# Pooled attention and a gated MLP: maxima of the late heads turned one head at a time, under a new order

## The chip, the cores and the metric

The kernel runs on one core of one Trainium2 chip, as one launch. The metric is the device time of a run in microseconds (us). Three runs of the kernel before gave 902.53, 903.97 and 904.75 us, a median of 903.97.

## The reference

The inputs are q, k and v (4 batches, 8 heads, 1152 positions, 64 channels, fp32) and the two weights of an MLP (512 x 2048 and 2048 x 512).

```python
q_pool = q.reshape(B, H, S // 2, 2, D).mean(axis=3)          # 576 pooled queries
scores = scale * np.matmul(q_pool, k.transpose(0, 1, 3, 2))  # 576 x 1152 per head
scores = scores - np.max(scores, axis=-1, keepdims=True)
attn = np.exp(scores)
attn = attn / (np.sum(attn, axis=-1, keepdims=True) + 1e-09)
x = np.matmul(attn, v)        # then heads side by side: 2304 x 512
h = x @ w_in
g = h * np.clip(h + 3.0, 0.0, 6.0) / 6.0
out = g @ w_out
```

The softmax needs the maximum of each pooled query over all 1152 keys. In the kernel the scores lie with the keys on the partitions and the queries along the free dimension, so this maximum runs over nine key tiles (elementwise, on VectorE) and then across the 128 partitions (which needs a transposition).

## The kernel before

**Tiling.** The heads are taken in pairs: 16 pairs `g`, four for each batch. A pair has two halves of 288 queries (`h`), and in each of these two heads (`j`). Pairs 0 to 4 (`g < EARLY`) are the first part: fp32 scores of both heads at once, in PSUM rooms called `v`. Pairs 5 to 15 are the late part: the scores are two matmuls of a split into a high and a low word, one head at a time. Beside the first part the MLP weights are converted from the raw words into a high and a low half (`convert`, L599, seven steps on ScalarE, GpSimd and VectorE for each of 32 pieces). The MLP takes the tokens in chunks of 256, 16 steps of the hidden dimension each. Six chunks lie among the late pairs; the last 768 tokens follow in a loop at the end (L866 on).

**The maximum of a late head.** `scores` (L398) leaves a key tile in PSUM. ScalarE copies it to the SBUF tile `s` (`keep`, L417), VectorE keeps the running maximum `m` (`most`, L424), 128 x 288 for each head. For the two heads of one `(g, h)` then follow, in the kernel before:

- `cross_m` (L431), ScalarE, once a head: 64 partitions of the head's `m` are copied into the other 64 partitions of a PSUM tile `pst`.
- `join_m` (L439), VectorE, once a head: the maximum of these and of the head's own 64 partitions, into `pm`. After both, `pm` holds head 0 in partitions 0 to 63 and head 1 in 64 to 127.
- `fold` (L444), TensorE, once for both heads: three transpositions of 128 x 96 of `pm` into `pst`.
- `best` (L450), VectorE, once for both: a maximum over 64 elements, six results to a partition, `mq`.
- `spread` (L457), TensorE, once a head: three transpositions that lay `mq` along the free dimension of all partitions, into a fresh `pst`.
- `lessen` (L467), VectorE, three a head: subtracts it from the 128 x 864 blocks of `s`. `expo` (L476), ScalarE, follows.

The early heads have no `cross_m` and `join_m`: `fold` and `best` run once a head on `m` itself, with a maximum over 128 elements and three results, and `spread` writes into the tile that `fold` used. The tile `pst` is one PSUM bank, `st` in the planner. The sums of the exponentials go another way (`total` L480, `cross_d` L504, `join_d` L511, `sums` L517): GpSimd adds, ScalarE carries one head's 64 partitions over, GpSimd joins.

**What sets the order.** The class `Order` (L37) is a planner that runs while the kernel is built. Each step has a place (a number that is its priority), the engines that may take it with a busy and an end time, steps that it needs, and rooms (buffers) that it takes and frees. The planner goes through time; a free engine takes, of the steps whose needs are met and whose rooms are free, the one with the lowest place. What it yields is the order of issue on every engine, TensorE, VectorE, ScalarE, GpSimd and the queue of SyncE (SP) that starts nearly all DMAs. Each engine then works through its own list in order. The places come from constants at L20 to L34: `PER` (places for one pair, early and late), `AT` and `ATL` (shifts of each kind of step, early and late), `CONV` and `CSTEP` (weight conversion), `START` and `SLOPE` (MLP chunks), `LAG` and `MLP` (steps inside the MLP), `BIAS` (how readily a step goes to its second engine). The planner's steps of the maximum are `mp`, `mc`, `s1`, `s2`, `s3`, `su` (L748 to L766). `second` (L815) is the border between the parts: it waits for all early scores and for the conversion of 12 of the 16 weight blocks.

Of the kernel before, what the change touches and what calls it, by code (L numbers as in the profile page):

```python
# [11 lines left out]
F32 = mybir.dt.float32  # L12
# [6 lines left out]


SBUFS = 3
START = (94.79, 128.23, 169.33, 204.1, 247.91, 270.62)
SLOPE = (2.19, 3.02, 2.72, 2.51, 1.78, 3.47)
LAG, MLP = 9.42, (2.56, -1.5, 4.75, 1.71)
CONV, CSTEP = 27.2, (39.17, 25.6)
NEAR = 5
EARLY, FCV = 5, 12
CVB = 1
BIAS = (-3.16, 165.7, 1.3, -2.73, 8.4, 2.65)
CUT = 8  # L30
PER = (18.24, 19.02)
AT = (1.82, 3.28, -1.17, 8.45, 1.17, 16.24, 17.65, 6.2, 8.03, -0.11, 4.3, 2.83, -21.04, 27.48)
ATL = (0.23, 5.42, -4.41, 15.94, 13.8, 18.37, 11.77, 34.99, -2.44, 15.27, 4.54, 6.0, -6.43, -6.01)
TAIL = 768  # L34


# [90 lines left out]
def pooled_attention_then_gated_mlp(ctx, tc, q, k, v, w_in, w_out, out):  # L127
# [128 lines left out]
    with ExitStack() as a:  # L256
# [171 lines left out]
        def halves(j):  # L428
            return slice(j * D, (j + 1) * D), slice((1 - j) * D, (2 - j) * D)

        def cross_m(eng, u):  # L431
            g, h, j = u
            if j == 0:
                st_t["x", g, h] = ps_st.tile([P, TQ * P], F32, tag="m", name="pst")
                m_t["p", g, h] = sm.tile([P, HQ], F32, tag="pm", name="pm", bufs=2)
            mine, other = halves(j)
            copy(eng, st_t["x", g, h][mine, 0:HQ], m_t[g, h][other, j])

        def join_m(eng, u):  # L439
            g, h, j = u  # L440
            mine, _ = halves(j)
            nc.vector.tensor_tensor(out=m_t["p", g, h][mine], in0=st_t["x", g, h][mine, 0:HQ], in1=m_t[g, h][mine, j], op=ALU.max)
# [236 lines left out]
        room = dict(kr=1, qr=1, qp=1, vr=2, kT=2, v=3, q=2, mb=2, pm=2, dh=2, s=3, S=SBUFS, m=2, st=1, d=2, av=1, x=2, xo=2,  # L679
                    raw0=1, raw1=1, size0=1, size1=1, wd0=1, wd1=1, mx=2, w0=3, w1=3, h=1, r6=2, g=3, o0=1, o1=1, ob=2)  # L680
        od = Order(room)
        add = od.add
# [6 lines left out]
        for g in range(NG):  # L689
# [34 lines left out]
            for h in range(NH):  # L724
                for j in range(2):
                    u = (g, h, j)
                    z0 = place(g) + UNIT * (2 * h + j)
                    tag = "s" if late else "v"
                    if late or j == 0:
                        before = (g, h, 0) if j else (g, h - 1, late) if h else (g - 1, NH - 1, g - 1 >= EARLY) if g else None  # L730
                        for t in range(KT):
                            end = t == KT - 1
                            z = z0 + UNIT / KT * t * (1 if late else 2)
                            add(("mm", u, t), z, {"PE": (268, 480) if late else (760, 980)}, partial(scores, u=u, t=t),
                                ([("mm", u, t - 1)] if t else [("mm", before, KT - 1)] if before else [])
                                + ([("ql", g, h, j) if late else ("qh", g, 0, 0)] if not t else []) + [("kl", g, t // KC) if late else ("kh", g, t // 6)]
                                + ([("second",)] if late and not t else []),
                                (tag,), (("q",) * (j if late else h) + ("kT",) * (h == NH - 1 and j == late)) if end else ())
                            first = not t and not j
                            add(("cp", u, t), z, {"ACT": (300, 400) if late else (505, 605)}, partial(keep, u=u, t=t),  # L740
                                [("mm", u, t)] + ([("cp", u, t - 1)] if t else []), ("S", "m") if first else (), () if t else (tag,))
                            if t:
                                add(("mx", u, t), z + .1, {"DVE": (368, 450) if late else (668, 750)}, partial(most, u=u, t=t),
                                    [("cp", u, t)] + ([("mx", u, t - 1)] if t > 1 else []), (), (tag,))
                    w = u if late else (g, h, 0)
                    last = [("mx", w, KT - 1)]
                    z = z0 + (UNIT if late or j else 2 * UNIT)
                    if late:  # L748
                        add(("mp", u), z + at[8], {"ACT": (300, 400)}, partial(cross_m, u=u), [("mx", (g, h, n), KT - 1) for n in range(2)] if late else last, () if j else ("pm", "st"))
                        add(("mc", u), z + at[8], {"DVE": (370, 450)}, partial(join_m, u=u), [("mp", u)] + [("mc", (g, h, 0))] * j, (), ("m", "st") if j else ())  # L750
                        if j:
                            p = (g, h)
                            add(("s1", p), z + at[2], {"PE": (330, 550)}, partial(fold, u=p), [("mc", (g, h, n)) for n in range(2)], ("st",), ("pm",))
                            add(("s2", p), z + at[2], {"DVE": (474, 550)}, partial(best, u=p), [("s1", p)], (), ("st",))
                            for n in range(2):
                                add(("s3", (g, h, n)), z + at[2] + n, {"PE": (250, 470)}, partial(spread, u=(g, h, n)), [("s2", p)] + [("s3", (g, h, 0))] * n, ("st",))
                    else:
                        add(("s1", u), z + at[2], {"PE": (330, 550)}, partial(fold, u=u), last, ("st",), ("m",) if j else ())
                        add(("s2", u), z + at[2], {"DVE": (474, 550)}, partial(best, u=u), [("s1", u)])
                        add(("s3", u), z + at[2], {"PE": (250, 470)}, partial(spread, u=u), [("s2", u)])  # L760
                        add(("sb", u), z + at[2], {"ACT": (300, 400)}, partial(keep_m, u=u), [("s3", u)], ("mb",))
                    for c in C3:
                        add(("su", u, c), z + at[3] + c, {"DVE": (970, 1045)} if late else {"DVE": (970, 1045), "POOL": (2000, 2050, BIAS[0])}, partial(lessen, u=u, c=c),
                            [("s3", u) if late else ("sb", u)] + ([("su", u, c - 1)] if c and late else []), (),
                            (("st",) if c == 2 else ()) if late else (("st", u, 3), ("mb", u, 3)))
                        add(("ex", u, c), z + at[3] + 1 + c, {"ACT": (831, 930)}, partial(expo, u=u, c=c), [("su", u, c)])  # L766
                    for n in range(4 if late else 0):
                        cost = 2000 if n < 2 else 765
                        add(("ad", u, n), z + at[4] + 1.5 * n, {"POOL": (cost, cost + 50)}, partial(total, u=u, n=n),
                            [("ex", u, c) for c in (range(2) if n == 0 else (2,) if n == 1 else ())] + ([("ad", u, n - 1)] if n else []),  # L770
                            () if n else ("d",), (("S", u[:2], 3),) if n == 1 else ())
                    if late:
                        add(("dx", u), z + at[7], {"ACT": (300, 400)}, partial(cross_d, u=u), [("ad", u, 3)], () if j else ("dh",))
                        add(("dj", u), z + at[7], {"POOL": (765, 815)}, partial(join_d, u=u), [("dx", u)], (), ("d",))
# [147 lines left out]
```

## Time and profile before

| what | value |
|---|---|
| median of 3 runs | 903.97 us |
| the profiled execution, its own time | 904.39 us |
| its span, first to last instruction | 902.5 us |
| mean granted clock of TensorE | 0.987 |
| TensorE matmuls busy (PE) | 863.0 us, 96% |
| TensorE weight loads busy (PEld) | 671.9 us, 74% |
| VectorE busy (DVE) | 638.4 us, 71% |
| ScalarE busy (ACT) | 618.4 us, 69% |
| GpSimd busy (POOL) | 523.4 us, 58% |

The profile is of one execution; 1.9 us of its time lie outside its span. Matmuls are pipelined and the end of one is modelled, so the busy time of PE is that of overlapping records; how closely the starts follow each other tells how full the engine is. The granted clock is given as a share of 2.4 GHz: a stretch at 1.00 ran at 2.4 GHz, one at 0.50 at 1.2 GHz, and a value between is a mean over both.

### The profile page before, as it was taken

The numbers are of one execution on the slowest core, as the hardware profiler recorded it, in microseconds if no ns is written. First come the engines' busy times: TensorE is split into PE (matmuls) and PEld (weight loads), VectorE is DVE, ScalarE is ACT, GpSimd is POOL, SyncE is SP. The second block draws the span as 40 slices with busy tenths as digits, with TensorE's granted clock in tenths as the row PEclk, the third lists the DMA queues.
The fourth block names the chain that finished last, engine by engine and source line by source line (L and its number), as shares of the span: only waits on it lengthen the run. The fifth ranks groups of instructions, "written<-read, shape, count | busy, mean of one in ns | idle before, by whom it ended". The sixth has DMA issues, their size and how long they took to land.

```text
span 902.5 us, 16987 instructions
## 1 busy us (share of the span) xinstructions
PE 863.0 (96%) x5976; PEld 671.9 (74%) x5976; DVE 638.4 (71%) x1196; ACT 618.4 (69%) x1320; POOL 523.4 (58%) x474
## 2 busy tenths in 40 slices
PE   4889989989999999999999999999999999999997
PEld 3445445457778887889888888888888877888886
DVE  5879989887898888777877777787876761322222
ACT  4878888875778888878777787787876763222222
POOL 2556747444567888867686977677885695000000
PEclk9889999999999999999999999999999999999999
DMA  9978576469988777769686787787678658534433
GB/s 261 277 225 257 201 232 218 156 205 303 323 273 276 222 234 207 245 218 320 213 246 214 223 280 236 266 273 250 221 262 273 198 189 282 181 121 135 138 96 93
DMA packets 113396, 204.00 MB, mean 226 GB/s; under 512 B 44448, under 2 KB 68000, under 8 KB 113312
## 3 DMA queue, kind: packets, MB, share of 16 engines
q1 hardware_dynamic: 112624, 201.55, 70.1%
q10 hardware_dynamic: 688, 1.38, 0.5%
q8 instruction: 47, 0.77, 0.4%
q14 instruction: 37, 0.30, 0.1%
HBM read 171.97 MB, written 30.93 MB: 225 GB/s over the span
## 4 chain that ended last, share of the span: by engine, by line
PE 75%; DMA 7%; DVE 7%; ACT 5%; issue 3%; POOL 2%; SPq 0%; DVEq 0%; ACTq 0%; POOLq 0%
PE ph L183 21%; PE po L216 16%; PE pav L495 12%; PE pqk L408 12%; PE pt L216 5%; DVE m L426 3%; DMA raw<-in_moe_w_in_dram 2%; DMA raw<-in_moe_w_out_dram 2%; PE pst L465 2%; ACT s L310 2%; PE pt L382 1%; DMA qr<-in_q_dram 1%; ACT s L478 1%; DMA w_d<-scratch 1%; PE psr L521 1%
## 5 line engine op out<-in xcount | busy, mean ns | idle before, releaser
L470 DVE TENSOR_TENSOR s<-s,pst 128x864 f32<-128x864 f32 x168 | 173.8, 1047 | 32.6 <-PE pst L465 27.4
L478 ACT ACTIVATE s<-s 128x864 f32<-128x864 f32 x192 | 176.7, 933 | 24.6 <-DVE s L470 22.6
L183 PE MATMUL ph<-mxmxh,w 128*128 128x256 f32 x896 | 181.0, 285 | 0.0
L426 DVE TENSOR_TENSOR m<-pqk,m 128x288 f32<-128x288 f32 x308 | 139.6, 453 | 38.2 <-ACT s L310 27.0
L495 PE MATMUL pav<-s,vr 128*64 128x288 f32 x1152 | 156.6, 417 | 0.0
L310 ACT COPY s<-pqk 128x288 f32<-128x288 f32 x396 | 145.9, 400 | 14.3 <-PE pqk L408 10.8
L183 PEld LDWEIGHTS ph<-mxmxh,w 128*128 128x128 f32 x896 | 146.5, 190 | 2.2 <-issue 0.9
L216 PE MATMUL po<-w,gh 128*128 128x512 f32 x448 | 139.3, 392 | 0.0
L188 ACT ACTIVATE r<-ph,three 128x256 f32<-128x256 f32 (+1 forms) x128 | 64.1, 501 | 102.1 <-PE ph L183 98.2
L183 PE MATMUL ph<-mxmxl,w 128*128 128x256 f32 x448 | 126.4, 282 | 0.0
L408 PE MATMUL pqk<-qh,kT 128*128 128x288 f32 x396 | 124.2, 327 | 2.2 <-DVE m L426 1.0
L488 POOL TENSOR_TENSOR d<-s 128x864 f32<-128x864 f32 x44 | 90.1, 2048 | 58.1 <-ACT s L478 55.2
L495 PEld LDWEIGHTS pav<-s,vr 128*64 128x64 f32 x1152 | 78.1, 138 | 59.1 <-issue 11.1
L192 DVE SCALAR_TENSOR_TENSOR r<-r,ph 128x256 f32<-128x256 f32 (+1 forms) x128 | 57.5, 449 | 90.2 <-ACT r L188 89.7
L408 PE MATMUL pqk<-ql,kT 128*128 128x288 f32 x396 | 111.6, 294 | 0.0
L201 POOL TENSOR_TENSOR gl<-r,gh 128x256 fp32r<-128x256 f32 x96 | 70.9, 738 | 52.1 <-ACT gh L196 34.1
L216 PEld LDWEIGHTS po<-w,gh 128*128 128x128 f32 x448 | 84.3, 188 | 14.5
L216 PE MATMUL po<-w,gl 128*128 128x512 f32 x224 | 90.0, 402 | 1.5 <-DMA w<-w_d 1.5
L488 POOL TENSOR_TENSOR d<-d,s 128x864 f32<-128x864 f32 x44 | 90.3, 2051 | 0.6
L408 PEld LDWEIGHTS pqk<-qh,kT 128*128 128x128 f32 x396 | 74.6, 188 | 17.8 <-DVE m L426 5.2
L183 PEld LDWEIGHTS ph<-mxmxl,w 128*128 128x128 f32 x448 | 85.2, 190 | 0.8
L196 ACT CAST gh<-r 128x256 fp32r<-128x256 f32 (+1 forms) x128 | 55.7, 435 | 39.3 <-DVE r L192 26.7
(97 smaller groups left out, 1500.7 us busy)
## 6 DMA issues: line engine op xcount, KB each, us to landing
w<-w_d SPq DMA_DIRECT2D x224, 512.0 KB, 5.0
w_d<-scratch SPq DMA_DIRECT2D x32, 512.0 KB, 5.5
kr<-in_k_dram SPq DMA_DIRECT2D x32, 288.0 KB, 5.0
vr<-in_v_dram SPq DMA_DIRECT2D x16, 576.0 KB, 4.0
qr<-in_q_dram SPq DMA_DIRECT2D x15, 576.0 KB, 6.8
raw<-in_moe_w_in_dram SPq DMA_DIRECT2D x16, 512.0 KB, 5.3
raw<-in_moe_w_out_dram SPq DMA_DIRECT2D x16, 512.0 KB, 5.1
xh_d<-xh SPq DMA_DIRECT2D x32, 144.0 KB, 4.8
```

The costliest lines, as they stand in the source:

```text
L183: nc.tensor.matmul(ps, w[:, wi, cs], x[:, c, :], start=(m == 0), stop=(m == 3 * NCC - 1))
L188: nc.scalar.activation(out=r6, in_=ps, func=AF.Relu, bias=three)
L192: nc.vector.scalar_tensor_tensor(out=out, in0=r6, scalar=6.0, in1=ps, op0=ALU.min, op1=ALU.mult)
L201: on.tensor_tensor(out=gl, in0=r6, in1=gh.bitcast(F32), op=ALU.subtract)
L216: nc.tensor.matmul(o, g[:, ts], w[:, wi, :], start=(f == 0 and n == 0), stop=(f == NFC - 1 and n == 2))
L310: nc.scalar.copy(out=out, in_=in_)
L408: nc.tensor.matmul(ps[:, 0:HQ], kT[g][:, j, t, :], w[:, j, :], start=(m == 0), stop=(m == 1))
L426: nc.vector.tensor_tensor(out=m, in0=ps, in1=s0 if t == 1 else m, op=ALU.max)
L470: by[eng].tensor_tensor(out=s, in0=s, in1=m.unsqueeze(1).to_broadcast([P, KC, HQ]), op=ALU.subtract)
L478: nc.scalar.activation(out=s, in_=s, func=AF.Exp, scale=SCALE)
L488: by[eng].tensor_tensor(out=out, in0=x, in1=y, op=ALU.add)
L495: nc.tensor.matmul(av_t[g, h][j * D:(j + 1) * D, :], vr_t[g][:, j, t, :], s_t[g, h][:, j, t, :], start=(t == 0), stop=(t == KT - 1),)
```

## The change

For the late pairs `cross_m` and `join_m` go, with their tiles. `fold`, `best` and `spread` are now the same for early and late: once a head, on `m` itself, and `spread` writes into the tile of `fold`. The sums of the two heads are still joined. All constants of the order are new; the costs in the planner are the same ones. The cut diff:

```diff
-START = (94.79, 128.23, 169.33, 204.1, 247.91, 270.62)
-SLOPE = (2.19, 3.02, 2.72, 2.51, 1.78, 3.47)
-LAG, MLP = 9.42, (2.56, -1.5, 4.75, 1.71)
-CONV, CSTEP = 27.2, (39.17, 25.6)
+START = (107.21, 129.44, 181.69, 204.5, 238.8, 274.39)
+SLOPE = (2.16, 3.08, 1.38, 1.98, 2.64, 2.75)
+LAG, MLP = 7.8, (2.55, -3.98, 15.46, 2.58)
+CONV, CSTEP = 20.06, (51.27, -5.14)
...
-BIAS = (-3.16, 165.7, 1.3, -2.73, 8.4, 2.65)
+BIAS = (-4.9, 201.89, 3.95, -7.11, 17.98, 9.02)
 CUT = 8
-PER = (18.24, 19.02)
-AT = (1.82, 3.28, -1.17, 8.45, 1.17, 16.24, 17.65, 6.2, 8.03, -0.11, 4.3, 2.83, -21.04, 27.48)
-ATL = (0.23, 5.42, -4.41, 15.94, 13.8, 18.37, 11.77, 34.99, -2.44, 15.27, 4.54, 6.0, -6.43, -6.01)
+PER = (18.27, 18.6)
+AT = (1.61, 2.63, -2.01, 12.09, -1.48, 16.23, 12.27, 2.3, 6.72, -1.57, 5.33, 2.34, -49.57, -29.1)
+ATL = (-0.35, 5.1, -1.26, 35.67, 13.02, 16.99, 7.49, 56.73, -0.96, 4.9, 4.35, 18.93, -19.18, -7.86)
...
-        def cross_m(eng, u):
...
-        def join_m(eng, u):
...
         def fold(eng, u):
             st = st_t[u] = ps_st.tile([P, TQ, P], F32, tag="m", name="pst")
-            m = m_t[u[:2]][:, u[2]] if len(u) > 2 else m_t.pop(("p",) + u)
+            m = m_t[u[:2]][:, u[2]].rearrange("p (t q) -> p t q", q=QP)
             for x in range(TQ):
-                nc.tensor.transpose(st[:QP, x, :], m[:, x * QP:(x + 1) * QP], ident)
+                nc.tensor.transpose(st[:QP, x, :], m[:, x, :], ident)
 
         def best(eng, u):
-            n = 1 if len(u) > 2 else 2
-            mq = sm.tile([QP, TQ * n], F32, tag=f"mq{n}", name="mq")
-            nc.vector.tensor_reduce(out=mq, in_=st_t[u][:QP].rearrange("p x (j k) -> p (x j) k", j=n), axis=AX.X, op=ALU.max)
-            for j in range(n):
-                m_t["q", u if n == 1 else u + (j,)] = mq[:, j::n]
+            m_t["q", u] = sm.tile([QP, TQ], F32, tag="mq", name="mq")
+            nc.vector.tensor_reduce(out=m_t["q", u], in_=st_t[u][:QP], axis=AX.X, op=ALU.max)
 
         def spread(eng, u):
             mq = m_t.pop(("q", u))
-            if u[0] < EARLY:
-                st = st_t[u].rearrange("p x k -> p (x k)")[:, 0:HQ]
-            else:
-                st = ps_st.tile([P, TQ * P], F32, tag="m", name="pst")[:, 0:HQ]
-            st_t[u] = st
+            st = st_t[u] = st_t[u].rearrange("p x k -> p (x k)")[:, 0:HQ]
...
-                    if late:
-                        add(("mp", u), z + at[8], {"ACT": (300, 400)}, partial(cross_m, u=u), [("mx", (g, h, n), KT - 1) for n in range(2)] if late else last, () if j else ("pm", "st"))
-                        add(("mc", u), z + at[8], {"DVE": (370, 450)}, partial(join_m, u=u), [("mp", u)] + [("mc", (g, h, 0))] * j, (), ("m", "st") if j else ())
-                        if j:
...
-                    else:
...
+                    add(("s1", u), z + at[2], {"PE": (330, 550)}, partial(fold, u=u), last, ("st",), ("m",) if j else ())
+                    add(("s2", u), z + at[2], {"DVE": (474, 550)}, partial(best, u=u), [("s1", u)])
+                    add(("s3", u), z + at[2], {"PE": (250, 470)}, partial(spread, u=u), [("s2", u)])
+                    if not late:
                         add(("sb", u), z + at[2], {"ACT": (300, 400)}, partial(keep_m, u=u), [("s3", u)], ("mb",))
```

## Rows read from the trace of the kernel before

**Rows 1.** The page: busy time, and 40 slices of 22.6 us

```profile
PE 863.0 (96%) x5976; PEld 671.9 (74%) x5976; DVE 638.4 (71%) x1196; ACT 618.4 (69%) x1320; POOL 523.4 (58%) x474
...
PE   4889989989999999999999999999999999999997
...
DVE  5879989887898888777877777787876761322222
...
PEclk9889999999999999999999999999999999999999
```

**Rows 2.** The stretches: us, busy of PE, PEld, DVE, ACT, POOL, granted clock, DMA

```profile
270.00:745.00 475.00, 474.35 (x3417) 398.85 (x3416) 367.04 (x731) 372.78 (x860) 364.06 (x324) 1.00 0.75 241
0.00:187.00 187.00, 159.89 (x1195) 86.25 (x1196) 158.54 (x255) 143.15 (x243) 100.85 (x92) 0.95 0.75 231
187.00:270.00 83.00, 78.20 (x579) 60.14 (x578) 71.75 (x136) 59.16 (x136) 46.88 (x46) 0.98 0.84 277
745.00:902.50 157.50, 150.54 (x791) 126.71 (x789) 41.07 (x76) 43.27 (x82) 11.65 (x14) 0.99 0.46 149
```

**Rows 3.** The timeline of TensorE around one fold: start, us, what

```profile
326.30 0.28 PE L183 MATMUL ph<-mxmxh,w 128*128 128x256 f32 x1
326.42 0.49 PE L448 MATMUL pst<-ident,pm 128*96 128x128 f32 x3
326.66 0.38 PE L408 MATMUL pqk<-qh,kT 128*128 128x288 f32 x1
326.88 0.29 PE L408 MATMUL pqk<-ql,kT 128*128 128x288 f32 x1
327.01 0.29 PE L408 MATMUL pqk<-qh,kT 128*128 128x288 f32 x1
```

**Rows 4.** The stretches of 10 us, TensorE alone: busy us, granted clock, DMA

```profile
10.00:20.00 10.00, 6.14 (x33) 0.93 1.12 279
20.00:30.00 10.00, 8.96 (x46) 0.73 1.12 316
30.00:40.00 10.00, 7.85 (x44) 0.83 0.88 296
...
60.00:70.00 10.00, 9.48 (x50) 0.68 0.65 192
...
190.00:200.00 10.00, 8.39 (x54) 0.83 0.48 136
```

**Rows 5.** The waits of TensorE from 26 to 70 us: total us, times, longest

```profile
PE psr L559 <- ACT rw L310: 2.4, 1, 2.4
PE pv L404 <- DVE m L426: 2.0, 1, 2.0
```

**Rows 6.** The waits of TensorE from 180 to 200 us

```profile
PE pt L382 <- DVE kT L367: 1.6, 1, 1.6
```

**Rows 7.** The chain that ended last, from 51 to 61 us: start, us, what

```profile
51.16 7.34 DMA raw<-in_moe_w_out_dram
...
60.07 0.41 ACT rw L310
...
60.52 0.74 PE psr L559 x3
```

**Rows 8.** The groups by line: count, busy us, mean ns, idle before

```profile
L453 DVE TENSOR_REDUCE mq<-pst 96x6 f32<-96x384 f32 (+1 forms) x42 | 23.0, 547 | 5.8 <-PE pst L448 5.6
...
L442 DVE TENSOR_TENSOR pm<-pst,m 64x288 f32<-64x288 f32 x44 | 20.0, 455 | 12.4 <-ACT pst L310 11.7
...
L310 ACT COPY pst<-m 64x288 f32<-64x288 f32 x44 | 17.5, 398 | 5.0 <-DVE m L426 3.9
...
L448 PE MATMUL pst<-ident,pm 128*96 128x128 f32 x66 | 11.0, 275 | 0.3 <-DVE pm L442 0.3
```

**Rows 9.** The waits of SyncE's DMA queue: total us, times, longest

```profile
SPq L304 <- PE pav L495: 35.1, 11, 5.7
```

More of the change, by code (lines that the diff above doesn't have):

```diff
@@ L429, in halves @@
             return slice(j * D, (j + 1) * D), slice((1 - j) * D, (2 - j) * D)
-        def cross_m(eng, u):
[L432 to L437, printed above, removed]
-        def join_m(eng, u):
-            g, h, j = u
-            mine, _ = halves(j)
-            nc.vector.tensor_tensor(out=m_t["p", g, h][mine], in0=st_t["x", g, h][mine, 0:HQ], in1=m_t[g, h][mine, j], op=ALU.max)
         def fold(eng, u):
             st = st_t[u] = ps_st.tile([P, TQ, P], F32, tag="m", name="pst")
-            m = m_t[u[:2]][:, u[2]] if len(u) > 2 else m_t.pop(("p",) + u)
+            m = m_t[u[:2]][:, u[2]].rearrange("p (t q) -> p t q", q=QP)
             for x in range(TQ):
-                nc.tensor.transpose(st[:QP, x, :], m[:, x * QP:(x + 1) * QP], ident)
+                nc.tensor.transpose(st[:QP, x, :], m[:, x, :], ident)
         def best(eng, u):
-            n = 1 if len(u) > 2 else 2
-            mq = sm.tile([QP, TQ * n], F32, tag=f"mq{n}", name="mq")
-            nc.vector.tensor_reduce(out=mq, in_=st_t[u][:QP].rearrange("p x (j k) -> p (x j) k", j=n), axis=AX.X, op=ALU.max)
-            for j in range(n):
-                m_t["q", u if n == 1 else u + (j,)] = mq[:, j::n]
+            m_t["q", u] = sm.tile([QP, TQ], F32, tag="mq", name="mq")
+            nc.vector.tensor_reduce(out=m_t["q", u], in_=st_t[u][:QP], axis=AX.X, op=ALU.max)
         def spread(eng, u):
             mq = m_t.pop(("q", u))
-            if u[0] < EARLY:
-                st = st_t[u].rearrange("p x k -> p (x k)")[:, 0:HQ]
-            else:
-                st = ps_st.tile([P, TQ * P], F32, tag="m", name="pst")[:, 0:HQ]
-            st_t[u] = st
+            st = st_t[u] = st_t[u].rearrange("p x k -> p (x k)")[:, 0:HQ]
             for x in range(TQ):
@@ L677, in load_last @@
                 nc.sync.dma_start(out=x[:, p, :].bitcast(F32), in_=d[p, :, NT - TAIL + CT:])
-        room = dict(kr=1, qr=1, qp=1, vr=2, kT=2, v=3, q=2, mb=2, pm=2, dh=2, s=3, S=SBUFS, m=2, st=1, d=2, av=1, x=2, xo=2,
+        room = dict(kr=1, qr=1, qp=1, vr=2, kT=2, v=3, q=2, mb=2, dh=2, s=3, S=SBUFS, m=2, st=1, d=2, av=1, x=2, xo=2,
                     raw0=1, raw1=1, size0=1, size1=1, wd0=1, wd1=1, mx=2, w0=3, w1=3, h=1, r6=2, g=3, o0=1, o1=1, ob=2)
@@ L747, in pooled_attention_then_gated_mlp @@
                     z = z0 + (UNIT if late or j else 2 * UNIT)
-                    if late:
-                        add(("mp", u), z + at[8], {"ACT": (300, 400)}, partial(cross_m, u=u), [("mx", (g, h, n), KT - 1) for n in range(2)] if late else last, () if j else ("pm", "st"))
-                        add(("mc", u), z + at[8], {"DVE": (370, 450)}, partial(join_m, u=u), [("mp", u)] + [("mc", (g, h, 0))] * j, (), ("m", "st") if j else ())
-                        if j:
[L752 to L756, printed above, removed]
-                    else:
-                        add(("s1", u), z + at[2], {"PE": (330, 550)}, partial(fold, u=u), last, ("st",), ("m",) if j else ())
-                        add(("s2", u), z + at[2], {"DVE": (474, 550)}, partial(best, u=u), [("s1", u)])
-                        add(("s3", u), z + at[2], {"PE": (250, 470)}, partial(spread, u=u), [("s2", u)])
+                    add(("s1", u), z + at[2], {"PE": (330, 550)}, partial(fold, u=u), last, ("st",), ("m",) if j else ())
+                    add(("s2", u), z + at[2], {"DVE": (474, 550)}, partial(best, u=u), [("s1", u)])
+                    add(("s3", u), z + at[2], {"PE": (250, 470)}, partial(spread, u=u), [("s2", u)])
+                    if not late:
                         add(("sb", u), z + at[2], {"ACT": (300, 400)}, partial(keep_m, u=u), [("s3", u)], ("mb",))
```

## The prediction

> **What bounds the kernel now.** I read the page first [rows 1]. TensorE is busy in 96% of the span and the next engine, VectorE, in 71%; but the 40 slices show two regimes. Up to slice 9 TensorE and VectorE are both at 7 to 9 tenths and the granted clock is below full in slices 2 and 3 (and once more in slice 9). From slice 13 to the last TensorE stands at 9, VectorE at 6 to 8, and the clock at 9.
>
> Then the stretches by stage [rows 2]. From 270 to 745 us TensorE is busy 474.35 of 475 us, with VectorE at 367.04, ScalarE at 372.78 and GpSimd at 364.06, all under 79%: there the work of TensorE alone sets the time. From 0 to 187 us TensorE is busy 159.89 and VectorE 158.54 of 187 us: 27.1 and 28.5 us of gaps, and no engine is the bound by itself. From 745 us on the attention is nearly over, and what follows is not touched by this change.
>
> A busy TensorE could still be a loosely filled one, since ends are modelled. So the timeline around a fold decides [rows 3]: starts follow each other by 0.12 or 0.13 us through layer and score matmuls, with no idle mark between pieces. The fold starts at 326.42 and its successor at 326.66. The queue is tight; what is added to it in this stage is paid for.
>
> Last the first part, with the clock [rows 4]: five stretches of 10 us have a granted clock of 0.93, 0.73, 0.83, 0.68 and 0.83, that is, shares of them at 1.2 instead of 2.4 GHz. Ahead of or in three of them stands a pause of TensorE: 2.0 us for a maximum and 2.4 us for a copy between 26 and 70 us [rows 5], 1.6 us for a key tile after 180 us [rows 6]. The chain shows where the 2.4 us come from [rows 7]: a raw weight load takes 7.34 us to land, ScalarE sits in order behind it, the copy of the reciprocals comes at 60.07 us, and TensorE goes on at 60.52, into the stretch at 0.68.
>
> **The change part by part.** There are 11 late pairs, 22 times two halves, so 22 groups `(g, h)` and 44 heads.
>
> Removed on ScalarE: 44 copies of 398 ns, 17.5 us. Removed on VectorE: 44 joins of 455 ns, 20.0 us; added there: 22 reductions of 547 ns (the row mixes the joined form and the early one, which read the same 96 x 384 elements), 12.0 us. VectorE so loses 8.0 us [rows 8]. Nearly all of this lies where TensorE is the bound, so I cost it at nothing. The cover is TensorE's own work. If it were gone, the most that could come back is the part between 187 and 270 us, where VectorE is busy 71.75 of 83 us [rows 2]: two or three of the 11 pairs, 3 x 0.7 = some 2 us at most.
>
> Added on TensorE: 22 folds of three transpositions. The price of one is read from the timeline [rows 3]: 0.24 us from its start to the next start, and the score matmul behind it then takes 0.22 us to its successor where the next one takes 0.13. That is 0.24 + 0.09 = 0.33 us, and 22 x 0.33 = 7.3 us. The ends: by the first gap alone 22 x 0.24 = 5.3 us (a fold that stands beside other transpositions shares the step); by the records' busy time, which counts overlap, 11.0 us for the 66 transpositions of the 22 folds now there [rows 8]. I take 7.3, since the starts set the pace of a full queue.
>
> [...]
>
> The spreads stay 44 and only write into the fold's tile. The new folds wait for the head's own last maximum where the joined fold waited for the join; queued behind a fold on TensorE are scores and layers, and behind these nearly everything. The folds now there cost 0.3 us of such idle time in all [rows 8], so twice as many cost some 0.3 more: nothing, with 2 us as an upper bound. The bank `st` is taken once a head and held through fold, reduction, spread and three subtractions, in place of twice for the maxima and once for each spread; both work out to a few microseconds a head in a period of some 11 us (475 us for fewer than 44 heads), so it isn't the bound.
>
> The new order: every early and late constant moves, but no work is added. In the first part the conversion has lower places, yet most of its pieces were already behind the attention (place 91 for the border) and served as filling. The loads of q and v get much lower places (for v +27.5 to -29.1 early): one DMA each per pair, which SP now issues as soon as their rooms are free, ahead of raw loads, conversion writes and weight loads. SP has stood 35.1 us in 11 waits for a v buffer to come free [rows 9], 3.2 us each; five early pairs more of that would hold raw loads back by up to 16 us, and TensorE only through a pause like the one at 58 us. I take nothing for it, and up to 6 us as the upper end: one new fall like that of 60 to 70 us, 2.4 us of pause and 10 x (1 - 0.68) = 3.2 us of clock.
>
> What can the new order give? The two later falls and their pauses are what another order can avoid: 3.2 + 1.7 us of clock [rows 4] and 2.4 + 1.6 us of pause [rows 5, 6], 8.9 us. The three before 40 us (0.7 + 2.7 + 1.7 us) lie in the opening, with the DMA share at 0.88 to 1.12. Time that TensorE gains becomes time of the kernel only as far as VectorE can follow, and its gaps are as large as TensorE's. With a bound of nothing (the pauses turn up elsewhere, as they came from a late DMA that no order foresees) and of 8.9 us, I take the middle, 4.4 us.
>
> Sum on the profiled execution: 904.4 + 7.3 - 4.4 = 907.3 us. It is 0.4 us over the median of the three runs, so against the median of 904.0 the forecast is **907.0 us**, slower by 0.3%. The main case's own range runs from 904.0 + 5.3 - 8.9 = 900.4 to 904.0 + 11.0 = 915.0.
>
> **The rivals.**
>
> *The first part gives back more than the folds cost.* If the new order fills the pauses, all five lows could go: 10.0 us of clock [rows 4] and 6.0 us of pauses [rows 5, 6], 16.0 us. Then 904.0 + 7.3 - 16.0 = 895.3 us. For it: 27.1 us of TensorE's gaps lie there [rows 2]. Against it: the opening is full of DMA, and VectorE is as busy. It decides from 10 us of gain on.
>
> *A new fall.* One more pause and low of the size of that at 60 us, and nothing gained: 904.0 + 7.3 + 5.6 = 916.9 us. For it: places of loads and conversion were moved, and the pause came from a raw load. Against it: the work is the same.
>
> *The folds fit into TensorE's places.* Then the first part's gain stands alone: 904.0 - 4.4 = 899.6 us. Against it stand the starts [rows 3]. [...]
>
> *The folds cost clock.* If the late stage, at a granted clock of 1.00 now [rows 2], had one low of the smaller size (1.7 us) with each pair, 11 x 1.7 = 18.7 us would come on top: 925.7 us. Against it, the stage already holds folds, spreads and turns of keys and queries without a low. [...]
>
> **How the numbers follow.** A measurement of this kernel can tell about 0.3%, 2.7 us, from no change: 901.3 to 906.7 counts as the same. Main case 0.48 (0.25 slower, 0.19 same, 0.04 faster, as it runs from 900.4 to 915.0); the first part gives more 0.25 (0.23 faster, 0.02 same); a new fall 0.17 (0.14 slower, 0.03 same); folds that fit 0.06 (half faster, half same); folds that cost clock 0.04 (slower). Together 0.30 faster, 0.27 same, 0.43 slower. The range reaches down to 896, nearly the whole of the first rival, and up to 914; the outer parts of the second rival and the last one are left out.
>
> **What would show it.** Right: in the late stage 44 folds of 0.24 us between starts, TensorE still without gaps, the stage longer by some 7 us, VectorE and ScalarE lower there by about 8 and 17 us; in the first part fewer lows, its end some 4 us earlier. Wrong: a late stage of the same length (then the folds were hidden), or a border before 180 us with the clock near 1.00 (then the first part gave more), or new waits of TensorE for a fold or a copy.

## The result, and the profile after

The changed kernel took 914.91 us (median of 7 runs, 908.52 to 919.22), the kernel before 904.75 us beside it (7 runs, 902.53 to 906.97): a ratio of **1.0113, interval 1.0089 to 1.0137**, 10.2 us slower. Slower was the likeliest sign in the forecast, but 907.0 us was the number, and 914.91 lies just above the range's upper end of 914.

The page of the changed kernel, in the lines that answer to [rows 1]:

```profile
span 913.1 us, 17092 instructions
...
PE 870.3 (95%) x6042; PEld 680.6 (75%) x6042; DVE 624.9 (68%) x1168; ACT 602.7 (66%) x1273; POOL 538.4 (59%) x483
...
PE   5788989999989999999999999999999999999997
...
DVE  4897889888897877776777767787767772222222
...
PEclk9898999999999999999999999999999999999999
```

VectorE is 13.5 us less busy than before and ScalarE 15.7 us, where the removed steps alone make 8 and 17.5; GpSimd is 15.0 us busier. TensorE has 66 records more (22 folds of three) and 7.3 us more of busy time. This looks like the plan; the span is 10.6 us longer all the same. So the next view is by stage, for the changed kernel (columns as in [rows 2]; 194.4 us is its first MLP matmul):

```profile
0.00:194.40 194.40, 164.44 (x1188) 87.86 (x1189) 156.37 (x252) 141.57 (x239) 108.02 (x99) 0.95 0.74 226
194.40:270.00 75.60, 70.57 (x535) 54.17 (x532) 65.55 (x122) 55.42 (x125) 52.34 (x48) 0.98 0.86 267
270.00:745.00 475.00, 474.98 (x3470) 403.95 (x3470) 356.22 (x711) 356.41 (x818) 359.64 (x319) 1.00 0.76 242
```

From 270 to 745 us TensorE is as full as it was (474.98 of 475 us, clock 1.00), and VectorE and ScalarE are 10.8 and 16.4 us lower. The time is not in a gap of this stage. Two milestones help to place it: the first start of an MLP layer matmul (`ph<-mxmxh`), which is the border between the parts, and the first start of the closing loop (`ph<-last`). Each line gives count, min/median/max ns, and first and last start. The kernel before:

```profile
L183 PE MATMUL ph<-mxmxh,w x896: 274/283/388, 188.2 to 880.5; 128*128 128x256 f32 x180
...
L183 PE MATMUL ph<-last,w x192: 387/389/497, 765.6 to 890.0; 128*128 128x512 f32 x192
```

The changed kernel:

```profile
L183 PE MATMUL ph<-mxmxh,w x896: 274/283/388, 194.4 to 891.3; 128*128 128x256 f32 x180
...
L183 PE MATMUL ph<-last,w x192: 389/389/503, 774.8 to 900.7; 128*128 128x512 f32 x192
```

The border moved from 188.2 to 194.4 us (+6.2), from there to the closing loop it is 580.4 instead of 577.4 us (+3.0), and the rest is 138.3 instead of 136.9 us (+1.4). **By this border more than half of the loss lies in the first part, where the code of the change adds nothing.** A border is a coarse measure, since it depends on how far the late pairs have come by then; the experiments show by how much. In the first part VectorE's waits differ. Its longest ones of the first 187 us, before (total us, times, longest):

```profile
DVE s L470 <- ACT mb L310: 4.7, 8, 1.5
DVE kT L312 <- PE pv L348: 4.3, 2, 3.8
DVE mq L453 <- PE pst L448: 3.7, 3, 1.8
DVE m L426 <- ACT s L310: 3.6, 6, 1.4
```

and after (the changed kernel is shorter, so its line numbers are lower: fold L435 for L448, reduction L439 for L453, subtraction L450 for L470, and the abs step of the conversion, which takes the absolute value of the raw words on ScalarE, L585 for L605):

```profile
DVE m L426 <- ACT s L310: 13.1, 16, 2.6
DVE mq L439 <- PE pst L435: 4.4, 5, 2.0
DVE kT L312 <- PE pv L348: 4.1, 3, 3.7
```

The running maximum waits 13.1 us instead of 3.6 us for ScalarE's copy of a score tile. VectorE's busy time in the first 187 us fell from 158.54 [rows 2] to 150.91 us: 7.6 us of work came later. ScalarE shows why the copies are late. The timelines of ScalarE and VectorE around one of the longest of these waits (in brackets: idle before, and what ended it):

```profile
122.86 0.64 ACT L310 COPY s<-pv 128x576 f32<-128x576 f32 x1
125.55 0.66 ACT L585 ACTIVATE scratch<-raw 128x512 f32<-128x512 f32 x1 [2.05 <-DMA raw<-in_moe_w_in_dram]
126.11 0.63 ACT L310 COPY s<-pv 128x576 f32<-128x576 f32 x1
...
126.77 0.76 DVE L426 TENSOR_TENSOR m<-pv,s 128x576 f32<-128x576 f32 x1 [2.57 <-ACT s L310]
```

ScalarE stands 2.05 us in the abs step, whose raw weights have not landed; the copy is next in its list, and VectorE's maximum stands 2.57 us for that copy. Of the nine longest such waits in the changed kernel six, 7.4 of the 13.1 us, have an abs step that waited 0.75 to 2.05 us for a raw load at most three instructions ahead of the copy. In two of the others ScalarE had stood in another step of the conversion, 1.43 us for VectorE and 1.62 us for a write of converted weights. ScalarE's waits for raw loads in the first 187 us were 3.9 + 2.8 us before (w_in + w_out) and 6.8 + 4.6 us after. The loads themselves are no slower: those of the first part landed after a median of 4.7 to 4.9 us in both.

### The profile page after: what moved, and what is told of

Its sections match the earlier page's. It is cut to its first block, busy times and chain, and to the rows that moved or that the text cites. A ratio compares the mean times of both kernels' runs of the same rounds, so it can differ in the third digit from the quotient of the medians.

```text
span 913.1 us, 17092 instructions
## 1 busy us (share of the span) xinstructions
PE 870.3 (95%) x6042; PEld 680.6 (75%) x6042; DVE 624.9 (68%) x1168; ACT 602.7 (66%) x1273; POOL 538.4 (59%) x483
## 4 chain that ended last, share of the span: by engine, by line
PE 74%; DVE 9%; DMA 8%; issue 3%; ACT 3%; POOL 2%; SPq 1%; DVEq 0%; ACTq 0%; POOLq 0%
PE ph L183 21%; PE po L216 16%; PE pav L475 12%; PE pqk L408 11%; PE pt L216 5%; DVE m L426 3%; DMA raw<-in_moe_w_in_dram 3%; DMA raw<-in_moe_w_out_dram 2%; PE pst L435 2%; DVE s L450 1%; DMA w_d<-scratch 1%; PE pst L445 1%; DMA w<-w_d 1%; PE pv L404 1%; PE pt L382 1%
## 5 line engine op out<-in xcount | busy, mean ns | idle before, releaser
L450 DVE TENSOR_TENSOR s<-s,pst 128x864 f32<-128x864 f32 x165 | 171.8, 1046 | 17.2 <-PE pst L445 15.9
L183 PE MATMUL ph<-mxmxh,w 128*128 128x256 f32 x896 | 181.1, 285 | 0.1
L404 PE MATMUL pv<-qh,kT 64*128 64x288 f32 x360 | 70.6, 495 | 8.0 <-DVE m L426 4.5
```

The source lines that it names most:

```text
L183: nc.tensor.matmul(ps, w[:, wi, cs], x[:, c, :], start=(m == 0), stop=(m == 3 * NCC - 1))
L404: nc.tensor.matmul(ps[:, j, 0:HQ], kT[g][d, t, :], q_t[g][d, h, :], start=True, stop=True)
L450: by[eng].tensor_tensor(out=s, in0=s, in1=m.unsqueeze(1).to_broadcast([P, KC, HQ]), op=ALU.subtract)
```

## The experiments

Each ratio is against the kernel before, run beside it, with its 95% interval. It is not the quotient of the two medians; where the two differ enough to matter, the text says so. "Old" and "new" constants are those of the two sides of the diff.

**Which part carries the time: four kernels that mix code and constants.** The first is the old code under all new constants.

```diff
-AT = (1.82, 3.28, -1.17, 8.45, 1.17, 16.24, 17.65, 6.2, 8.03, -0.11, 4.3, 2.83, -21.04, 27.48)
+AT = (1.61, 2.63, -2.01, 12.09, -1.48, 16.23, 12.27, 2.3, 6.72, -1.57, 5.33, 2.34, -49.57, -29.1)
...
```

> The kernel before (late maxima joined) under all constants of the changed one; its order in the first part is that of the changed kernel, row by row. Theory A (the 22 added folds cost TensorE 0.33 us each, 7.3 us, and the new first part costs the other 3 us through pauses and lows of the clock): about 3 us over the kernel before, 907 to 909 us, with a border near 194 us. Rival B (the folds are hidden, the order costs it all): about 10 us over it, as the changed kernel, 914 to 916. Rival C (the order is neutral, the head-by-head maxima cost 10 us): equal to the kernel before within 2 us.

Measured: 910.52 us, 1.0070 (1.0044 to 1.0095). The new order alone, with no fold added, is slower. Its border is at 194.2 us, that of the changed kernel.

The second is the old kernel and order, with each late fold's three transpositions done twice (22 folds more, as in the change; nothing removed).

```diff
-            for x in range(TQ):
+            for x in list(range(TQ)) * (1 if len(u) > 2 else 2):
```

> The kernel before with each joined fold of the late part issued twice into the same tile (the second writes the same values again); the order of all engines is unchanged, 22 folds of three transpositions are added as in the change, with no reduction, copy or join added or removed. Theory A: 7.3 us over the kernel before (5.3 to 11.0), all of it between 230 and 740 us. Rival B (TensorE has free places for them): within 1 us of the kernel before. Rival C (a fold costs more than its places on TensorE, by its wait): 7.3 us at most here, since the wait isn't doubled, so less than the change costs.

Measured: 907.55 us, 1.0059 (1.0032 to 1.0086): 5.3 us (2.9 to 7.8). The difference of the medians is only 1.9 us (905.68 us before) and that of the means 3.9 us, so the folds cost time, but how much is known no better than to a factor of two or three. The late stage of this kernel (columns as in [rows 2]):

```profile
270.00:745.00 475.00, 474.64 (x3446) 401.34 (x3445) 364.58 (x726) 369.87 (x854) 360.05 (x320) 1.00 0.75 239
```

Weight loads fill 401.34 of 475 us, 84%, and yet added transpositions cost time. The granted clock stays at 1.00. A doubled fold in TensorE's timeline:

```profile
324.06 0.82 PE L448 MATMUL pst<-ident,pm 128*96 128x128 f32 x6
324.63 0.38 PE L408 MATMUL pqk<-qh,kT 128*128 128x288 f32 x1
```

Six transpositions take 0.57 us from start to next start, where the three of [rows 3] took 0.24: the added triple takes 0.33 us. Over the 22 folds of the late part this time is 12.9 us here and 5.9 us in the kernel before, 7.0 us more.

The third is the changed code and its late constants, with the old early ones (`PER[0]`, `AT`, `BIAS`, `CONV`, `CSTEP`).

```diff
-AT = (1.61, 2.63, -2.01, 12.09, -1.48, 16.23, 12.27, 2.3, 6.72, -1.57, 5.33, 2.34, -49.57, -29.1)
+AT = (1.82, 3.28, -1.17, 8.45, 1.17, 16.24, 17.65, 6.2, 8.03, -0.11, 4.3, 2.83, -21.04, 27.48)
...
```

> The changed kernel (head by head) with the first part's constants of the kernel before (PER early, AT, CONV, CSTEP, BIAS) and the new ones for the late part and the MLP; the order of the first part is that of the kernel before. Theory A: 7.3 us over the kernel before, 911 to 913 us, and 3 us under the changed one, with a border near 188 us. Rival B: equal to the kernel before within 2 us. Rival C: as the changed kernel, 914 to 916.

Measured: 904.48 us, 0.9998 (0.9980 to 1.0017). **Under the old first part the head-by-head maxima cost nothing.** The border is back at 187.5 us.

The fourth is the old code with the old early and the new late constants.

```diff
-ATL = (0.23, 5.42, -4.41, 15.94, 13.8, 18.37, 11.77, 34.99, -2.44, 15.27, 4.54, 6.0, -6.43, -6.01)
+ATL = (-0.35, 5.1, -1.26, 35.67, 13.02, 16.99, 7.49, 56.73, -0.96, 4.9, 4.35, 18.93, -19.18, -7.86)
...
```

> The kernel before (joined) with its own first part and the new constants for the late part and the MLP. Theory A (TensorE is full in the late part under either order, so the late order is worth nothing): equal to the kernel before within 2 us. A rival in which the new late order costs something by itself: 3 us or more over it. One in which the late order gains: 3 us or more under it, and a version faster than both.

Measured: 906.04 us, 1.0011 (0.9986 to 1.0036). On the old code the late constants are worth nothing that can be seen. Of the four corners (the changed kernel, measured apart from the other three, is one), both with the old early constants stand at 1.00, both with the new ones at 1.007 and 1.011: the early constants cost 0.6% on the old code and 1.15% on the new. Read the other way, the head-by-head code costs nothing under the old first part and 0.4% under the new one; the last figure is hardly clear of noise (1.0044 to 1.0095 against 1.0089 to 1.0137).

**What the removed work was worth.** The old kernel without the 44 copies and 44 joins; the fold reads head 0's maxima, and so it no longer waits for those of head 1. It leaves out the maxima of head 1.

```diff
-            copy(eng, st_t["x", g, h][mine, 0:HQ], m_t[g, h][other, j])
+            pass
...
-            m = m_t[u[:2]][:, u[2]] if len(u) > 2 else m_t.pop(("p",) + u)
+            m = m_t[u[:2]][:, u[2] if len(u) > 2 else 0]
```

> The kernel before with the 44 copies of ScalarE and the 44 joins of VectorE left out (the joined fold reads head 0's maxima alone, so head 1's are not taken into account); TensorE's work and all orders else are unchanged. Theory F (the late part loses time at score matmuls that wait for their PSUM room, and 17.5 us of ScalarE and 20 us of VectorE less shorten these waits): 4 to 8 us under the kernel before, 898 to 902 us, with the gain between 188 and 766 us. Rival G, the prediction's own step (TensorE is full there, the removed work is hidden): within 1 us of the kernel before.

Measured: 900.56 us, 0.9963 (0.9937 to 0.9989): 3.3 us back (1.0 to 5.7). So ScalarE's and VectorE's work beside a full TensorE, with the hand-overs that hang on it, was not free. One place to look is TensorE's weight loads between 270 and 745 us. They waited for a score room that VectorE's maximum frees, in the kernel before:

```profile
PEld pqk L408 <- DVE m L426: 3.1, 11, 0.4
```

and in the changed one:

```profile
PEld pqk L408 <- DVE m L426: 0.9, 2, 0.4
```

In the kernel without copies and joins it is 2.2 us in 8 waits, but in the one with doubled folds, where nothing was taken away, 1.9 us in 7. So these waits do not explain the 3.3 us; by which way they come back is not shown.

**The raw loads: a second buffer, and other places for the step that waits.** First the changed kernel with two raw tiles taken in turn. The order on all engines is the same; only a load's wait for its buffer goes. That wait stands in the queue of SyncE, which in the changed kernel waited 36.8 us in the first 187 us for VectorE's last step on the raw words (L602):

```profile
SPq L570 <- DVE scratch L602: 18.4, 12, 4.2
SPq L565 <- DVE scratch L602: 18.4, 9, 4.1
```

The edit:

```diff
-        raw = wr.tile([P, 4 * DM], U32, tag="a", name="raw")
+        raw = [wr.tile([P, 4 * DM], U32, tag=t, name="raw") for t in "ac"]
...
-            r = raw[:, 2 * DM * half:2 * DM * (half + 1)]
+            r = raw[f % 2][:, 2 * DM * half:2 * DM * (half + 1)]
...
```

> The changed kernel with two buffers in place of one for the raw weight words (even and odd blocks); the order of every engine and of the DMA queue is row by row that of the changed kernel, but the queue no longer waits for the conversion of the block before, so the raw loads start and land earlier. Theory D (in the new first part the first conversion step stands on ScalarE just ahead of score copies and waits for raw loads in flight, 11.4 us; VectorE's maxima wait for the copies behind it, 13.1 us): these two waits go to under 3 us each, the border comes some 6 us earlier, near 188 us, and the time is 5 to 8 us under the changed kernel, 907 to 910 us. Rival E (the new first part is longer by its engines' work and order, the raw loads only fill its gaps): within 2 us of the changed kernel, with the border near 194 us.

Measured: 907.57 us, 1.0037 (1.0017 to 1.0056), so 0.75% off the changed kernel, and a border at 189.9 us. Time and border are as theory D had them, the waits are not: ScalarE's for raw loads fell only from 11.4 to 7.1 us and VectorE's for copies only from 13.1 to 11.6. In SP's list the waits for the raw tile fell from 36.8 to 3.2 us, but those for the converted weights that it writes (L612) rose from 30.3 to 50.9. By this one profile, then, VectorE's waits for copies are not the way by which most of the gain came; which one is, is open.

The same edit in the kernel with the old first part:

> The same second buffer in the kernel that is head by head under the old first part and the new late part (e4_headwise_early_old); its order is unchanged. There ScalarE waits 7.2 us for raw loads up to 187 us, but VectorE waits only 2.9 us for score copies, so theory D gives 1 to 3 us under the kernel before, 901 to 904 us, a version faster than both if it holds. Rival E: equal to the kernel before within 1 us.

Measured: 901.17 us, **0.9960 (0.9943 to 0.9978)**, faster than the kernel before (904.25 us beside it) and than the changed one. The second buffer also helps the old order, by 0.4%, though VectorE's waits for copies are 4.0 us here and 2.9 us without it. (The old code with two raw tiles was not tried, so how much of this is due to the head-by-head maxima is open.)

Next, the changed kernel with the planner's landing time of a raw load raised towards what the profile shows (medians of 5.1 and 5.4 us).

```diff
-                add(("lr", f, h), z - 8, {"SP": (470, 3000, 1550)}, ...
+                add(("lr", f, h), z - 8, {"SP": (470, 5300, 1550)}, ...
```

> The changed kernel with one cost of the planner changed: a raw load is taken to land 5.3 us after its issue, as measured, in place of 3.0 us, so the planner puts the conversion's first step where the load has landed; the constants are the same, the order is another one. Theory D: ScalarE's waits for raw loads and VectorE's for copies fall by half or more, the border comes before 191 us, 3 to 8 us under the changed kernel. Rival E: within 2 us of the changed kernel.

Measured: 918.00 us, 1.0157 (1.0130 to 1.0184). A miss: it makes another order altogether (border at 200.7 us). ScalarE's waits for raw loads are down to 4.7 us, and VectorE's waits for copies are 14.7 us all the same.

Then the changed kernel with each abs step of the first part moved behind the next two instructions of ScalarE (the step that follows it on GpSimd after it), the rest of the order kept:

```diff
+                i = at["cv", f, h, 0]
+                follow = [n for n in range(i + 1, at["cv", f, h, 2]) if todo[n][2] == "ACT"][:2]
...
+            put[i], put[clamp] = last + 0.3, max(clamp, last + 0.6)
```

> The changed kernel with one thing moved by hand: on ScalarE the first conversion step of the first part (which waits for the raw load) goes behind the two instructions that follow it, mostly score copies; TensorE, VectorE, GpSimd (but for one pair) and the DMA queue keep their order. Theory D (score copies stand behind that wait, and VectorE's maxima behind the copies): VectorE's wait for copies up to 187 us falls from 13.1 to under 7 us, the border comes 2 to 5 us earlier, and the time is 3 to 6 us under the changed kernel, 909 to 912 us. Rival E (that wait only fills time that the first part loses anyway): within 2 us of the changed kernel. A third way: the conversion itself becomes later and sets the border, 2 us or more over it.

Measured: 913.39 us, 1.0078 (1.0052 to 1.0105), with the border at 193.8 us: 1.5 us under the changed kernel by the medians and 0.35% by the ratios, which does not decide between theory D and rival E. VectorE's waits in the first 187 us (one line was added ahead, so lines are one higher):

```profile
DVE pv L594 <- POOL scratch L588: 7.1, 8, 1.9
DVE m L427 <- ACT s L311: 7.0, 17, 1.2
```

ScalarE's waits for raw loads fell from 11.4 to 2.6 us and VectorE's for copies from 13.1 to 7.0 us, but a new wait of 7.1 us came for the conversion's own next step (1.5 us in the changed kernel). The lateness went to another place in VectorE's list.

The same move in the best kernel (old first part, two raw tiles):

> The same move in the fastest kernel so far (head by head, old first part, new late part, two raw buffers). There VectorE waits 4.0 us for copies in the first part, so theory D leaves at most 2 us to gain: 899 to 902 us. Rival E: equal to that kernel, 901 us; the third way: 903 us or more.

Measured: 905.89 us, 1.0004 (0.9985 to 1.0023), 0.4% worse than without it, with the same new wait (7.2 us). Here ScalarE no longer waits for raw loads at all, and the third way of the expectation is what happened: the move makes the conversion late.

**Which constant.** By the planner's lists (none of this was run), the new places of the loads alone change only SP's list, and those of the conversion change, on the engines, the order of its last four blocks alone. Among the constants that change more is the fourth of `AT`, the place of the early subtractions. That one alone made new in the kernel with the old first part:

```diff
-AT = (1.82, 3.28, -1.17, 8.45, ...
+AT = (1.82, 3.28, -1.17, 12.09, ...
```

> The kernel that is head by head under the old first part and the new late part (equal to the kernel before), with one early constant set to its new value: the place of the early subtractions, 8.45 to 12.09. (Of the others, those of the loads, the conversion and the engines' biases leave the order of TensorE, VectorE and ScalarE as it is, row by row.) Theory H (later subtractions are what makes the new first part slow): most of the 10 us between that kernel and the changed one, 910 to 915 us, with a border after 191 us. Rival I (no single place is to blame; each change of a place gives another order, and the old one is simply among the good ones): 904 to 909 us.

Measured: 915.44 us, 1.0087 (1.0054 to 1.0121), 10 us by the medians; the border is at 208.2 us. One constant costs 0.9%. Its waits show the same picture as the changed kernel's. VectorE:

```profile
DVE m L426 <- ACT s L310: 13.8, 14, 2.4
```

and ScalarE:

```profile
ACT scratch L585 <- DMA raw<-in_moe_w_in_dram: 10.0, 4, 2.9
ACT scratch L585 <- DMA raw<-in_moe_w_out_dram: 8.2, 5, 2.5
```

The kernel with the old value had 2.9 us of the first and 3.7 + 3.5 us of the others.

That one alone put back in the changed kernel (12.09 to 8.45):

> The changed kernel with that one constant set back, 12.09 to 8.45. Theory H: near the kernel before, 904 to 907 us. Rival I: anywhere between 905 and 915 us, without relation to what the opposite step does in e13_early_old_su_later.

Measured: 910.11 us, 1.0050 (1.0029 to 1.0071), 0.6% off the changed kernel; about half of the early constants' cost. VectorE still waits 10.9 us for copies, and ScalarE 6.3 + 5.6 us for raw loads, as much as in the changed kernel. So this constant is enough to make the loads late, but the other early ones keep them late without it.

**Raw loads that are never late.** Two explanations were left: ScalarE stands behind late raw loads, or the later subtractions make copies late by themselves. These three kernels take these waits away with order, loads and their number unchanged (0.3 us is left in the third): all blocks are converted from the words of the first, and the other loads go to a tile that nobody reads. They leave out the weights of the other blocks. As with the second buffer, SP no longer waits for the raw tile either.

```diff
-            r = raw[:, 2 * DM * half:2 * DM * (half + 1)]
+            r = raw[min(f, 1)][:, 2 * DM * half:2 * DM * (half + 1)]
...
-            word = raw[:, 2 * DM * half:2 * DM * (half + 1)].rearrange("p (n two) -> p n two", two=2)
+            word = raw[0][:, 2 * DM * half:2 * DM * (half + 1)].rearrange("p (n two) -> p n two", two=2)
```

The changed kernel:

> The changed kernel, with the raw loads of all blocks but the first put into a second tile that nobody reads; every block is converted from the words of the first. So the loads stay in place and in number, no step on ScalarE waits for one, and the order of all engines is as it was. It leaves out the weights of all blocks but the first. Theory 'ScalarE stands behind late raw loads': the 1.1% over the kernel before is those waits, and this kernel is as fast as the next one of this call (old first part, same edit) within 0.3%, both near 0.995 of the kernel before. Theory 'the order itself': VectorE waits for copies that come late whatever ScalarE waits for; this kernel stays 0.6% or more over the next one, at 1.002 or more of the kernel before.

Measured: 900.53 us, 0.9972 (0.9957 to 0.9987). Its milestones:

```profile
L183 PE MATMUL ph<-mxmxh,w x896: 274/283/415, 181.1 to 877.1; 128*128 128x256 f32 x180
...
L183 PE MATMUL ph<-last,w x192: 388/389/501, 761.0 to 886.6; 128*128 128x512 f32 x192
```

The border comes at 181.1 instead of 194.4 us; from there to the closing loop it is 579.9 us, against 580.4. By the border of these two profiles nearly all of the gain, 13.3 us, lies in the first part. What is left of VectorE's wait for copies:

```profile
DVE m L426 <- ACT s L310: 6.2, 10, 1.8
```

The kernel with the old first part:

> The heads one by one under the old first part, with the same edit of the raw loads: the point that the other two of this call are compared with. Both theories: 0.993 to 0.997 of the kernel before, as the second raw buffer alone gave 0.996; if it gives more than that, raw loads were also late with two buffers.

Measured: 896.24 us, 0.9931 (0.9910 to 0.9952); the border is at 183.0 us, and it is 577.1 us from there to the closing loop.

The old first part with the later subtractions:

> The kernel with the old first part and only the early subtractions moved later (8.45 to 12.09; 1.0087 of the kernel before), with the same edit of the raw loads. Late raw loads as the cause: it falls to within 0.4% of the one ahead of it. The order itself: it stays 0.6% or more over it, so at about 1.002 of the kernel before.

Measured: 900.10 us, 0.9972 (0.9954 to 0.9990).

So neither explanation holds alone. The distance between new and old first part falls from 1.15% (1.0113 and 0.9998) to 0.41% (0.9972 and 0.9931), and that of the one constant from 0.89% to 0.41%. **Raw loads that hold an engine or the queue up carry some 0.7 of the 1.15 points; some 0.4 points (about 4 us) stay with the order.** By the intervals the 0.7 may be 0.3 to 1.1 and the 0.4 may be 0.15 to 0.7. The edit takes two waits away at once: ScalarE's for the loads (11.4 us in the changed kernel, 7.2 us under the old first part) and SP's for the raw tile (36.8 and 43.3 us), behind which other transfers stand in SP's list. To which of them the 0.7 belongs is not separated. What makes the 0.4 is open. The borders do not place it: with the new first part the border is no later (181.1 against 183.0 us) and the time from there to the closing loop 2.8 us longer, while with the one constant, in as much time, the border is 9.7 us later (192.7 us) and the time from there 9.4 us shorter (567.7 us).

## Why the prediction was right and wrong

**What bounds the late stage: right.** TensorE is full there after the change too, at a clock of 1.00.

**"The price of one is read from the timeline": right within the noise.** The 22 folds measured 5.3 us (2.9 to 7.8), and 7.3 us was the forecast. From the starts of the folds to the next starts, the trace has 7.0 us more (and 6.8 us in the kernel with 44 separate folds under the old first part). So 7.3 was a good price of the folds in TensorE's queue, though the run does not measure it closely; that the 5.3 us equal 22 x 0.24 is chance, as an added triple takes 0.33 us. The Trainium skill, "Perfetto Trace Analysis", section "Identifying the Most-Contended Engine", has TensorE's headroom judged by its arithmetic throughput (MFU) and the busy share of weight loads. That share alone, 84% here, did not tell that added transpositions would cost time; the starts did. The rival in which the folds cost clock falls with the 1.00 of the late stage under 44 folds.

**"Nearly all of this lies where TensorE is the bound, so I cost it at nothing": wrong.** Taking the copies and joins away gave 3.3 us (1.0 to 5.7); that the cap of 2 us was exceeded is likely and not certain. The step that failed is the cover: TensorE's records leave no gap in this stage, and work taken from other engines still gave time back, by a way that the traces do not show. With the folds' 5.3 us that makes a net cost of some 2 us for head-by-head turning. Measured under the old first part it is none, 0.9998 against 1.0011, a difference known to some 0.3%, about 3 us; within the noise the two agree.

**"What can the new order give?", 4.4 us back: wrong in sign; this is the step that failed most.** On the old code, with no fold added, the new order cost 0.70%, 6.3 us (4.0 to 8.6); on the new code the early constants cost 1.15%, 10.4 us. With the 6.3 us, the folds' 5.3 and the 3.3 given back the sum is 8.3 of the 10.2 us measured. I counted the pauses and falls that another order could avoid, bounded the gain below by nothing, and priced what it can lose only in a rival, at one pause. The 40 slices and the stretch of [rows 2] had said it: VectorE busy 158.54 of 187 us and ScalarE 143.15, with no engine the bound, is a stage in which a late hand-over between two engines can cost time. The chain [rows 7] even held the mechanism, a raw load of 7.34 us with ScalarE in order behind it. I took it for one pause to be filled, and did not ask how many other copies stand behind abs steps. In the changed order ScalarE waited 11.4 us for raw loads where it had waited 6.7, and VectorE 13.1 us for ScalarE's copies where it had waited 3.6; with no raw load late and no wait for the raw tile, that order is 1.4% faster (0.9972 against 1.0113) and the old one 0.7% (0.9931 against 0.9998). The sign that the prediction named, an end of the first part some 4 us earlier, came out as 6.2 us later.

**Moves of loads and conversion: nothing, not tested.** By the planner's lists the new places of the loads change SP's list alone, and no run has them alone. In the first 187 us SP waited 32.5 us for rooms of k, q and v (L294, L299, L304), where it had waited 21.7; the raw loads land as fast once they are issued, but whether they were issued later by this is open. What is enough by itself to make ScalarE wait longer for them is another constant of the first part, the place of the subtractions, which the prediction did not look at. How a later subtraction does that was not followed through the lists.

**The rivals.** "A new fall", 916.9 us, came nearest, and for a part of its reason: a raw load that ScalarE stands behind. The way it took, one pause of TensorE and one fall, is not what the traces show; VectorE's 16 waits of up to 2.6 us are. But the clock has a part. The two profiles show 0.986 against 0.987, and the kernel before is low there: its thirty executions beside the first four experiments have a median of 0.9915, the seven of the changed kernel 0.986. Among those thirty, 0.01 of mean clock goes with some 5 us, so by this estimate some 3 us of the 10 go with a lower clock. Whether that is a cause or comes of the waits is not shown. "The first part gives more" and "the folds fit" did not happen.

## What to carry to other kernels

Where no engine is the bound, a new order has a risk as large as its chance: count, for each instruction that waits for a DMA, what stands behind it in its engine's list and who waits for that, and bound the order's effect by a loss as well as by a gain. A change that comes with a new order is two changes; here the code cost nothing under the old order and perhaps 0.4% under the new one, the early order 0.6% to 1.15%, and old code under the new order and new code under the old one told them apart. A second buffer for loads that an in-order engine waits for was worth 0.4% to 0.75% without touching the order.

## What the runs showed of the hardware that was not expected

The lows of the clock are not a property of the order alone. Thirty executions of the kernel before, beside the first four experiments, have a mean clock of 0.983 to 0.998 and take 900.75 to 911.29 us. Three of these kernels have the same first part, and their profiles give three pictures of it: a mean clock of 0.995 with the border at 187.2 us (folds doubled), 0.987 with 188.2 us (the kernel before), and 0.981 with 194.9 us (without copies and joins, in the longest of its twelve runs, 908.32 us). A table of lows from a single profile, from which the prediction took its 8.9 us, says little of what an order can gain. It also limits what one border can show: the changed kernel's 194.4 us alone would prove nothing, and it is the times of many runs that put most of the loss on the early constants.
